# A fourth PSUM bank for the first experts' chunk, and squares of y that read SBUF

## The chip, the cores and the metric

One core of one Trainium2 chip. The metric is device time in microseconds (us) of one execution; the median of three runs of the kernel before is 762.8 us (761.18 to 762.97). Engines: PE is TensorE, DVE is VectorE, ACT is ScalarE, POOL is GpSimd, SP is SyncE, which issues nearly all DMAs.

## What is computed

```python
def reference(q, k, v, M_prev, z_prev, beta, w_in, w_out, domain_probs, w1, w2):
    # B, H, S, D = 2, 8, 576, 64
    attn = g * mem_out + (1 - g) * softmax(causal(q @ k.T / 8)) @ v     # g = sigmoid(beta)
    x = attn.transpose(0, 2, 1, 3).reshape(1152, 512)
    y = relu(x @ w_in) ** 2 @ w_out                                      # 512 -> 2048 -> 512
    p = domain_probs / domain_probs.sum(-1, keepdims=True)
    return sum(p[:, e:e+1] * (relu(y @ w1[e]) @ w2[e]) for e in range(4))  # 512 -> 1024 -> 512
```

## The kernel before, in words

The 1152 tokens are nine tiles of 128. The feed-forward layer in the middle (`ffn1`) takes them in three chunks: two tiles (c = 0), four tiles (c = 1), three tiles (c = 2). While chunk 0 runs, the attention of the other tiles is finished in between (`mix`), and so on; chunk 2 runs with the preparation of the experts. The values are kept as a high part and a low part (`xy[:, 0]`, `xy[:, 1]`), and products take three passes, high by high, high by low, low by high.

In `ffn1` the hidden units go in 16 blocks `f`: `up(f)` makes `hp` (12 matmuls, L89), ACT and DVE make the squared ReLU (L676, L677) and split it (L679, L680), `down(f)` adds to four PSUM accumulators `yacc` (L687). Behind the last block each accumulator is copied to `xy` by ACT (L693: the high part), subtracted by DVE (L694: the low part), and its squares are summed by ACT (L696, into `ysq`), from which a power-of-two scale for the experts is made later.

The experts are two chunks: c = 0 with tiles 0 to 3, c = 1 with tiles 4 to 8; each goes through 4 experts in 4 pairs of blocks, 16 pairs per chunk (`pairs`). A pair's first layer, `up2(i)`, is a seven-product (Strassen) form: for k = 0, 1, 4, 3, 5, 2, 6 in this order, `product(k)` makes six matmuls into one PSUM bank (L895), and ACT (L918, L924: k = 0 and 3) or DVE (L916, the other five) reads it. `hidden` then makes the ReLU's high part on ACT (L910) and its low part on DVE (L911). The second layer, `down2(i - 1)`, of the pair before is mixed in between: eight groups of three matmuls (L989) into the accumulators `o`. The order is two products, then a group of `down2`, a product, and so on. So each pair's first `down2` group needs the first `hidden` of the pair before, which comes from product 2, the last but one.

Which bank a product gets is set by `bank`: a counter goes up by one at each call, and its rest by three picks one of three PSUM tiles of one buffer each. A product can start when the product three calls before has been read. The two small sums `yt` and `wt` (L773) take a turn in the same rotation. The other five of the eight banks are `o0` to `o4`, in a pool `ps_o` that opens behind the first layer; the first expert chunk, of four tiles, uses `o0` to `o3`.

TensorE's instructions stand in the order in which the program writes them. Those of ACT, DVE, POOL and SP are put in order by a scheduler of the framework when the kernel is built, from its own estimates, so an edit can change their order far away from it. Each engine runs its instructions strictly in that order, and a wait blocks all behind it.

Of the kernel before, what the change touches and what calls it, by code (L numbers as in the profile page):

```python
# [10 lines left out]
F32 = mybir.dt.float32  # L11
# [5 lines left out]
AF = mybir.ActivationFunctionType  # L17
# [4 lines left out]
P = 128  # L22
B, H, S, D = 2, 8, 576, 64
DM = 512
NK = DM // P
# [27 lines left out]
def attention_then_experts(ctx, tc, qa, ka, va, qc, kc, vc, mz, beta, w1, probs, w2, out):  # L53
# [11 lines left out]
    nc = tc.nc  # L65
# [6 lines left out]
    ps_h = ctx.enter_context(tc.tile_pool(name="ps_h", bufs=1, space=PSUM))  # L72
# [5 lines left out]
    xy = xyp.tile([P, 2, NK, NTOK], F32R, name="xy")  # L78
# [41 lines left out]
    ysq = const.tile([P, 3, NK], F32, name="ysq")  # L120
# [3 lines left out]
    gp = kvs.enter_context(tc.tile_pool(name="gp", bufs=2))  # L124
# [516 lines left out]
    def ffn1(c, ps, gp, nh, cv=None):  # L641
        t0, t1 = CHUNKS[c]
        n, cs = (t1 - t0) * P, slice(t0 * P, t1 * P)
# [12 lines left out]
        def prep(f, half):  # L656
            if c == 0:
                while (f, half) not in made:
                    next(cv)
                raw = made.pop((f, half))  # L660
                next(cv, None)
            else:
                fetch(1)
                raw = raws.pop((f, half))
            w = wp.tile([P, 2, DM], F32R, tag=f"w{half}", name=f"w{half}")
            on_vector = ((f % 4 == 3, f % 4 == 3), (f < 3, f % 4 == 3), (False, f % 2))[c][half]
            split(w, raw, nc.vector if on_vector else nc.gpsimd)
            ws[f, half] = w
            fetch(2)
# [13 lines left out]
        def down(f):  # L683
            w, g = ws.pop((f, 1)), gs.pop(f)
            for d in range(NK):
                for i, (a, b) in enumerate(PASS):
                    nc.tensor.matmul(  # L687
                        yacc[d], lhsT=w[:, a, d * P:(d + 1) * P], rhs=g[:, b],
                        start=(f == 0 and i == 0 and d % per == 0),
                        stop=(f == n1 - 1 and i == 2 and d % per == per - 1),  # L690
                    )
                for k in range(d - per + 1, d + 1) if f == n1 - 1 and d % per == per - 1 else ():
                    nc.scalar.activation(out=xy[:, 0, k, cs], in_=yacc[k], func=AF.Copy)  # L693
                    nc.vector.tensor_sub(xy[:, 1, k, cs], yacc[k], xy[:, 0, k, cs].bitcast(F32))  # L694
                    junk = gp.tile([P, n], F32, tag="r", name="junk")
                    nc.scalar.activation(out=junk, in_=yacc[k], func=AF.Square, accum_out=ysq[:, c, k:k + 1])  # L696
                yield

        prep(0, 0)
# [2 lines left out]
        yacc = [banks[d // per][:, d % per, :] for d in range(NK)]  # L702
        for f in range(n1 + 2):
            if f + 1 < n1:
                prep(f + 1, 0)
            if 1 <= f <= n1:
                prep(f - 1, 1)
            if f < n1:
                yield from up(f)
            if f >= 2:  # L710
                yield from down(f - 2)

    with ExitStack() as ca:
        kva = ca.enter_context(tc.tile_pool(name="kva", bufs=1))
# [38 lines left out]
    ps_e = ctx.enter_context(tc.tile_pool(name="ps_e", bufs=1, space=PSUM))  # L753
    pairs = [(c, e, p) for c in range(2) for e in range(ne) for p in range(4)]
    width = [(t1 - t0) * P // 2 for t0, t1 in EXPERT_CHUNKS]
    xs, raws, wus, wds, gs = {}, {}, {}, {}, {}
    turn = [0]
# [3 lines left out]
    wsq = xp.tile([P, ne, 2, 4], F32, name="wsq", bufs=1)  # L761
    junk2 = xp.tile([P, 2 * DM], BF16, name="junk2", bufs=1)

    def bank(shape, name):
        turn[0] += 1
        pool, tag = ((ps_h, "h"), (ps_e, "b"), (ps_e, "d"))[turn[0] % 3]
        return pool.tile(shape, F32, tag=tag, name=name)

    def whole_sum(out, parts, acc):
# [74 lines left out]
    def fetch(i, half):  # L844
        if i < len(pairs):
            _, e, p = pairs[i]
            raw = raws[i, half] = xp.tile([P, 2 * DM], F32, tag=f"raw{half}", name=f"raw{half}", bufs=6 + half)
            nc.sync.dma_start(out=raw, in_=w2[e * 4 + p, half])
# [114 lines left out]
    ps_o = ctx.enter_context(tc.tile_pool(name="ps_o", bufs=1, space=PSUM))  # L963
# [45 lines left out]
                r += n  # L1009

    side = iter(())
    for i in range(len(pairs)):

        fetch(i + 6, 0)
        fetch(i + 6, 1)
        todo = iter([(j, half) for j in {0: (), 1: (4, 5), 2: (6, 7)}.get(i, (i + 5,)) for half in range(2)])
        if i:
            late = [down2(i - 1)] * (2 * (EXPERT_CHUNKS[pairs[i - 1][0]][1] - EXPERT_CHUNKS[pairs[i - 1][0]][0]))
            steps = spread([up2(i)] * 7, late, 0.25)
        else:  # L1020
            steps = []
        ahead = chain(prep_down(i), prep_up(i + 1))
        for n, g in enumerate(steps):
            next(g)
            next(ahead, None)
            if n in (5, 7, 9, 11):
                square(*next(todo, (len(pairs), 0)))
            if n == 10 and i == 1:
                y_power(1, bank([P, NK], "yt"))
                side = tokens(1, nc.vector)  # L1030
            if n == 14 and i < 4 * ne - 4 and i % 4 == 2:
                w_power(pairs[i + 2][1], bank([P, 8], "wt").rearrange("p (m n) -> p m n", m=2))
        if i >= 5 and steps:
            next(side, None)
        run(ahead)
# [61 lines left out]
```

## Time and profile before

| | |
|---|---|
| median of three runs | 762.8 us |
| the profiled execution | 762.13 us, its span from first to last instruction 760.1 us |
| PE busy | 706.0 us (93%) |
| DVE busy | 584.4 us (77%) |
| ACT busy | 448.6 us (59%) |
| POOL busy | 293.6 us (39%) |
| mean granted TensorE clock | 0.974 of full |

The span has these stretches: attention and first-layer chunk 0 to 152 us; chunk 1 with the last attention tiles to 301; chunk 2 with the experts' preparation to 389; experts' chunk 0 to 555; experts' chunk 1 to the end. Matmuls are pipelined, so PE's busy time is a union that covers overlaps; where PE was idle, the list of waits says what it waited for. The granted clock is 1.00 at 2.4 GHz and 0.50 at 1.2 GHz.

### The profile page before, as it was taken

To read this page: it belongs to the slowest core of one execution; us is meant where nothing else is said; L and a number is where in the kernel's file an instruction comes from. 1 tells how busy PE (TensorE), PEld (TensorE's weight loads), DVE (VectorE), ACT (ScalarE), POOL (GpSimd) and SP (SyncE) were. 2 spreads that over 40 slices of the span, in tenths; PEclk is the share of its full clock that TensorE was granted. 3 is DMA by queue.
4 is the path that set the end of the run, shared out by engine and by line. 5 is a ranking of instruction groups with operands and counts; after the bars stand their busy time and mean duration, and the time that the engine had idled before them with its cause. 6 is when DMAs were issued, how large, how long until landed. Compare 5 with 4: busy or idle time off the path is not lost.

```text
span 760.1 us, 12986 instructions
## 1 busy us (share of the span) xinstructions
PE 706.0 (93%) x4740; PEld 511.6 (67%) x4740; DVE 584.4 (77%) x1082; ACT 448.6 (59%) x878; POOL 293.6 (39%) x293
## 2 busy tenths in 40 slices
PE   6969999979999998989989898989999999999997
PEld 4758888867777886978866555656655555555553
DVE  4789998889989865566777679988777776776763
ACT  4679988785765545586766557645543534435341
POOL 1136645454533246744531324533333142332400
PEclk9979999999999999999989999999999999999999
DMA  9568776287885543685412322332333323100002
GB/s 241 172 231 281 245 249 231 91 272 215 178 209 125 114 111 91 209 289 167 139 57 66 101 88 87 104 108 92 124 121 113 92 75 111 56 1 1 1 1 69
DMA packets 65424, 101.28 MB, mean 133 GB/s; under 512 B 32656, under 2 KB 34704, under 8 KB 65360
## 3 DMA queue, kind: packets, MB, share of 16 engines
q1 hardware_dynamic: 65216, 100.45, 43.5%
q8 instruction: 37, 0.61, 0.3%
q14 instruction: 27, 0.22, 0.1%
q10 hardware_dynamic: 144, 0.00, 0.0%
HBM read 82.87 MB, written 10.75 MB: 123 GB/s over the span
## 4 chain that ended last, share of the span: by engine, by line
PE 55%; DVE 21%; ACT 9%; issue 7%; POOL 3%; DMA 3%; SPq 1%; DVEq 0%; POOLq 0%; ACTq 0%
PE o L989 18%; PE pe L895 16%; PE y L687 6%; PE hpb L89 3%; PE hpc L89 3%; DVE wu L859 2%; DVE bits L634 2%; PE pv L555 2%; DVE bits L631 2%; DVE a L172 2%; POOL w L83 1%; PE hpa L89 1%; PE sc L487 1%; PE sc L278 1%; DMA raw<-in_w 1%
## 5 line engine op out<-in xcount | busy, mean ns | idle before, releaser
L989 PE MATMUL o<-w,g 128*128 128x512 f16 x864 | 220.4, 383 | 6.2 <-ACT junk L696 2.2
L895 PE MATMUL pe<-xs,wu 128*128 128x256 f16 (+1 forms) x1344 | 200.6, 289 | 5.8 <-DVE h L916 5.7
L895 PEld LDWEIGHTS <-wu 128*128 128x128 f16 x1344 | 132.5, 99 | 76.6 <-issue 9.8
L989 PEld LDWEIGHTS <-g 128*128 128x128 f16 x864 | 84.8, 99 | 76.9 <-issue 4.3
L687 PE MATMUL y<-g,w 128*128 128x256 f32 (+2 forms) x576 | 124.1, 348 | 1.3 <-POOL w L83 0.7
L83 POOL TENSOR_TENSOR w<-wraw,w 128x512 fp32r<-128x512 f32 x49 | 72.2, 1475 | 107.2 <-ACT w L82 106.1
L910 ACT ACTIVATE g<-h 128x512 f16<-128x512 f32 (+1 forms) x64 | 43.4, 678 | 108.6 <-DVE h L916 108.4
L687 PEld LDWEIGHTS y<-g,w 128*128 128x128 f32 x576 | 93.8, 190 | 11.7 <-POOL w L83 0.9
L925 POOL TENSOR_TENSOR u<-u,p 128x256 f32<-128x256 f32 (+1 forms) x32 | 30.2, 944 | 126.2 <-ACT p L924 115.9
L862 POOL TENSOR_TENSOR ws<-raw 128x256 f32<-128x256 f32 x32 | 24.7, 772 | 117.5 <-issue 89.9
L911 DVE SCALAR_TENSOR_TENSOR g<-h,g 128x512 f16<-128x512 f32 (+1 forms) x64 | 50.5, 788 | 21.9 <-ACT g L910 21.7
L916 DVE SCALAR_TENSOR_TENSOR h<-pe,u 128x256 f32<-128x256 f32 (+1 forms) x96 | 43.1, 451 | 24.9 <-PE pe L895 17.9
L89 PE MATMUL hpb<-xy,w 128*128 128x512 f32 x192 | 53.9, 417 | 7.5 <-DVE r L677 5.8
L859 DVE SCALAR_TENSOR_TENSOR wu<-ws,wpow,wu 128x512 f16<-128x512 f32 x64 | 50.0, 819 | 3.6 <-ACT wu L870 3.6
L795 DVE SCALAR_TENSOR_TENSOR w<-raw,wpow,w 128x512 f16<-128x512 f32 x64 | 48.1, 754 | 0.7 <-ACT w L794 0.6
L89 PEld LDWEIGHTS hpb<-xy,w 128*128 128x128 f32 x192 | 36.5, 198 | 17.3 <-DVE r L677 8.3
L172 DVE CUSTOM_DVE_ANT_0 a<-sc,mask 128x384 f32<-128x384 f32 (+4 forms) x80 | 36.4, 476 | 13.4 <-PE sc L487 6.5
L89 PE MATMUL hpc<-xy,w 128*128 128x384 f32 x192 | 40.9, 361 | 6.1 <-POOL w L83 2.5
L82 ACT ACTIVATE w<-wraw 128x512 fp32r<-128x512 f32 x64 | 39.6, 624 | 11.0 <-PE y L687 8.8
L83 POOL TENSOR_TENSOR w<-bits,w 128x512 fp32r<-128x512 f32 x24 | 35.4, 1480 | 25.4 <-ACT w L82 25.4
L794 ACT ACTIVATE w<-raw,wpow 128x512 f16<-128x512 f32 x64 | 45.1, 709 | 0.1
L89 PE MATMUL hpa<-xy,w 128*128 128x256 f32 x192 | 35.7, 313 | 7.5 <-ACT mag L627 7.5
(160 smaller groups left out, 1268.6 us busy)
## 6 DMA issues: line engine op xcount, KB each, us to landing
raw<-in_w SPq DMA_DIRECT2D x64, 512.0 KB, 3.5
w<-in_w SPq DMA_DIRECT2D x32, 512.0 KB, 4.4
wraw<-w1s SPq DMA_DIRECT2D x64, 256.0 KB, 2.9
w1s<-bits SPq DMA_DIRECT2D x32, 256.0 KB, 2.4
kraw<-in_kc SPq DMA_DIRECT2D x8, 576.0 KB, 4.1
vraw<-in_vc SPq DMA_DIRECT2D x8, 320.0 KB, 3.4
qraw<-in_qc SPq DMA_DIRECT2D x4, 512.0 KB, 4.2
out<-acc SPq DMA_DIRECT2D x8, 256.0 KB, 2.1
```

The costliest lines, as they stand in the source:

```text
L83: eng.tensor_sub(w[:, 1], raw, w[:, 0].bitcast(F32))
L89: nc.tensor.matmul(acc, lhsT=w[:, a, kk * P:(kk + 1) * P], rhs=xy[:, b, kk, t0:t0 + n], start=(i == 0), stop=(i == 3 * NK - 1),)
L172: nc.vector.tensor_tensor_reduce(out=dst, in0=sc, in1=msk, op0=ALU.add, op1=ALU.max, scale=1.0, scalar=-3.0e38, accum_out=m)
L687: nc.tensor.matmul(yacc[d], lhsT=w[:, a, d * P:(d + 1) * P], rhs=g[:, b], start=(f == 0 and i == 0 and d % per == 0), stop=(f == n1 - 1 an ...
L794: nc.scalar.activation(out=w0, in_=x, func=AF.Copy, scale=s)
L795: nc.vector.scalar_tensor_tensor(out=w1, in0=x, scalar=s, in1=w0, op0=ALU.mult, op1=ALU.subtract)
L859: nc.vector.scalar_tensor_tensor(out=w[:, 1, ks], in0=x, scalar=s1, in1=w[:, 0, ks], op0=ALU.mult, op1=ALU.subtract)
L895: nc.tensor.matmul(acc, lhsT=w[:, wa, k, kk * P:kk * P + P], rhs=x[:, xb, kk], start=(m == 0), stop=(m == 5))
L910: nc.scalar.activation(out=g[:, 0], in_=hm, func=AF.Relu)
L911: nc.vector.scalar_tensor_tensor(out=g[:, 1], in0=hm, scalar=0.0, in1=g[:, 0], op0=ALU.max, op1=ALU.subtract)
L916: nc.vector.scalar_tensor_tensor(out=out, in0=acc, scalar=HID, in1=x, op0=ALU.mult, op1=ALU.add)
L989: nc.tensor.matmul(outs[t], lhsT=g[:, gb, r:r + P], rhs=w[:, wa], start=(p == 0 and m == 1 and k == 0), stop=(p == 3 and m == 0 and k == 2),)
```

## The change

The squares leave the loop over the accumulators and come behind it, as the last thing of the chunk; they read the high part of y in SBUF in place of the accumulator in PSUM. And the rotation gets a fourth tile, `o4` of `ps_o`, from the first pair of the expert loop until the second chunk begins.

```diff
                 for k in range(d - per + 1, d + 1) if f == n1 - 1 and d % per == per - 1 else ():
                     nc.scalar.activation(out=xy[:, 0, k, cs], in_=yacc[k], func=AF.Copy)
                     nc.vector.tensor_sub(xy[:, 1, k, cs], yacc[k], xy[:, 0, k, cs].bitcast(F32))
-                    junk = gp.tile([P, n], F32, tag="r", name="junk")
-                    nc.scalar.activation(out=junk, in_=yacc[k], func=AF.Square, accum_out=ysq[:, c, k:k + 1])
                 yield
...
             if f >= 2:
                 yield from down(f - 2)
+        for k in range(NK):
+            junk = gp.tile([P, n], F32, tag="r", name="junk")
+            y = xy[:, 0, k, cs].bitcast(F32)
+            nc.scalar.activation(out=junk, in_=y, func=AF.Square, accum_out=ysq[:, c, k:k + 1])
...
+    spots = [(ps_h, "h"), (ps_e, "b"), (ps_e, "d")]
+
     def bank(shape, name):
         turn[0] += 1
-        pool, tag = ((ps_h, "h"), (ps_e, "b"), (ps_e, "d"))[turn[0] % 3]
+        pool, tag = spots[turn[0] % len(spots)]
         return pool.tile(shape, F32, tag=tag, name=name)
...
     side = iter(())
+
+    spots.append((ps_o, "o4"))
     for i in range(len(pairs)):
+        if pairs[i][0] and len(spots) > 3:
+            spots.pop()
```

TensorE's order is the same in both kernels. The scheduler's order changes on the other engines; in the changed kernel the squares are line 713, and lines behind it have other numbers (L910 is L914, L911 is L915, L918 is L922, L864 is L868).

On ACT, at the end of first-layer chunk 1 (y_1997 to y_2000 are the four accumulators, tp a transposed tile of attention whose copy L199 the next chunk's first product reads; L82 copies a weight):

```order
 L693 ACTIVATE xy<-y_1997 128x512
+L713 ACTIVATE junk,ysq<-xy 128x512
 L693 ACTIVATE xy<-y_1998 128x512
 L693 ACTIVATE xy<-y_1999 128x512
-L696 ACTIVATE junk,ysq<-y_1997 128x512
-L696 ACTIVATE junk,ysq<-y_1998 128x512
-L696 ACTIVATE junk,ysq<-y_1999 128x512
 L199 ACTIVATE xy<-tp 128x4x128
 L693 ACTIVATE xy<-y_2000 128x512
+L713 ACTIVATE junk,ysq<-xy 128x512 x3
 L82 ACTIVATE w_3780<-wraw 128x512
-L696 ACTIVATE junk,ysq<-y_2000 128x512
```

Three squares stood ahead of the copy of tp; one stands there now, between the first two accumulators, and three stand behind the last accumulator's copy, ahead of the weight.

On ACT, at the end of first-layer chunk 2 and the start of the experts, the kernel before (y_3706 to y_3709 are the accumulators, g the first pair's hidden parts, p of pe a product's copy, wu weights):

```order
L693 ACTIVATE xy<-y_3706 128x384
L696 ACTIVATE junk,ysq<-y_3706 128x384
L910 ACTIVATE g_4506<-h_4428 128x512
L693 ACTIVATE xy<-y_3707 128x384
L910 ACTIVATE g_4524<-h_4427 128x512
L693 ACTIVATE xy<-y_3708 128x384
L693 ACTIVATE xy<-y_3709 128x384
L696 ACTIVATE junk,ysq<-y_3707 128x384
L918 ACTIVATE p_4582<-pe 128x256
L864 ACTIVATE wu<-raw_3874,wpow 128x768
L696 ACTIVATE junk,ysq<-y_3708 128x384
L696 ACTIVATE junk,ysq<-y_3709 128x384
```

and the changed kernel in the same place:

```order
L693 ACTIVATE xy<-y_3706 128x384
L713 ACTIVATE junk,ysq<-xy 128x384
L693 ACTIVATE xy<-y_3707 128x384
L914 ACTIVATE g_4504<-h_4428 128x512
L713 ACTIVATE junk,ysq<-xy 128x384
L693 ACTIVATE xy<-y_3708 128x384
L693 ACTIVATE xy<-y_3709 128x384
L914 ACTIVATE g_4520<-h_4427 128x512
L713 ACTIVATE junk,ysq<-xy 128x384 x2
L922 ACTIVATE p_4582<-pe 128x256
L868 ACTIVATE wu<-raw_3874,wpow 128x768
```

The last reading of an accumulator on ACT was a square behind a product's copy and a weight's; it is now the copy of y_3709, and the last two squares stand ahead of the product's copy.

On DVE, early in first-layer chunk 1 (L677 reads hpb and makes the squared ReLU, L166 and L167 belong to the attention's phi, L447 to its keys kst, L466 to its values vct):

```order
 L680 TENSOR_TENSOR g<-r,g 128x512
+L677 SCALAR_TENSOR_TENSOR r<-hpb,r 128x512
 L166 TENSOR_SCALAR phi<-phi 128x1024
-L677 SCALAR_TENSOR_TENSOR r<-hpb,r 128x512
 L167 SCALAR_TENSOR_TENSOR qraw<-qraw,phi 128x1024
-L466 SCALAR_TENSOR_TENSOR vct<-vraw,vs,vct 128x640
-L680 TENSOR_TENSOR g<-r,g 128x512
-L466 SCALAR_TENSOR_TENSOR vct<-vraw,vs,vct 128x640
-L447 TENSOR_TENSOR kst<-kraw,kst 64x576
+L680 TENSOR_TENSOR g<-r,g 128x512
+L466 SCALAR_TENSOR_TENSOR vct<-vraw,vs,vct 128x640 x2
 L677 SCALAR_TENSOR_TENSOR r<-hpb,r 128x512
```

One L677 moves ahead of L166, and the next L677 ahead of a subtraction for the keys. Some 20 rows further on both orders run alike again.

## Rows read from the trace of the kernel before

**Rows 1.** PE's list of waits: waiter, releaser, us in total, times, longest.
```profile
PE pe L895 <- DVE h L916: 5.7, 7, 1.6
...
PE o L989 <- DVE g L911: 2.1, 5, 0.9
...
PE hpb L89 <- ACT junk L696: 1.4, 1, 1.4
```

**Rows 2.** Windows: length, busy PE PEld DVE ACT POOL, granted clock, DMA share, GB/s.
```profile
450.00:490.00 40.00, 37.26 (x238) 23.80 (x237) 39.85 (x73) 27.29 (x45) 16.38 (x17) 0.96 0.31 97
510.00:750.00 240.00, 240.00 (x1458) 142.44 (x1457) 175.34 (x293) 105.45 (x162) 72.29 (x97) 1.00 0.20 66
```

**Rows 3.** The same view, of stretches right behind single waits of PE.
```profile
392.20:395.60 3.40, 3.40 (x13) 1.62 (x12) 2.62 (x7) 0.31 (x1) 0.75 (x2) 0.51 0.52 160
303.50:306.90 3.40, 3.40 (x12) 3.40 (x11) 0.81 (x2) 0.69 (x2) 0.00 (x0) 0.50 0.46 136
504.90:508.30 3.40, 3.09 (x12) 1.72 (x12) 3.33 (x14) 1.51 (x3) 0.00 (x0) 0.50 0.02 5
436.40:439.80 3.40, 3.40 (x22) 2.13 (x23) 3.40 (x7) 3.19 (x7) 0.00 (x0) 1.00 0.00 0
```

**Rows 4.** Timeline, chunk 1 begins: start, length, instruction, idle before and its releaser.
```profile
164.15 1.04 ACT L164 ACTIVATE phi<-qraw 128x1024 f32<-128x1024 f32 x1
165.10 0.58 ACT L676 ACTIVATE r<-hpb 128x512 f32<-128x512 f32 x1
166.15 0.69 DVE L166 TENSOR_SCALAR phi<-phi 128x1024 f32<-128x1024 f32 x1
167.49 4.35 PE L89 MATMUL hpb<-xy,w 128*128 128x512 f32 x12 [2.71 <-DVE r L677]
...
174.73 1.72 DVE L447 TENSOR_TENSOR kst<-kraw,kst 64x576 fp32r<-64x576 f32 x1
177.22 1.65 PE L89 MATMUL hpb<-xy,w 128*128 128x512 f32 x3 [1.57 <-DVE r L677]
```

**Rows 5.** Timeline where chunk 1 ends and chunk 2 begins.
```profile
300.07 0.59 ACT L696 ACTIVATE junk<-y 128x512 f32<-128x512 f32 x1
301.78 0.61 ACT L199 ACTIVATE xy<-tp 128x512 fp32r<-128x512 f32 x1
302.45 0.44 PE L89 MATMUL hpc<-xy,w 128*128 128x384 f32 x1 [1.77 <-ACT xy L199]
```

**Rows 6.** Timeline where chunk 2 ends and the experts begin.
```profile
389.02 1.01 DVE L694 TENSOR_TENSOR xy<-y,xy 128x384 fp32r<-128x384 f32 x2
390.86 0.53 ACT L696 ACTIVATE junk<-y 128x384 f32<-128x384 f32 x1
391.53 0.81 PE L989 MATMUL o<-w,g 128*128 128x512 f16 x3 [2.23 <-ACT junk L696]
```

**Rows 7.** Timeline between the tenth and the eleventh expert pair of chunk 0.
```profile
503.03 0.41 DVE L916 SCALAR_TENSOR_TENSOR h<-pe,u 128x256 f32<-128x256 f32 x1
503.49 0.81 PE L895 MATMUL pe<-xs,wu 128*128 128x256 f16 x6 [1.23 <-DVE h L916]
504.13 0.69 DVE L911 SCALAR_TENSOR_TENSOR g<-h,g 128x512 f16<-128x512 f32 x1 [0.70 <-ACT g L910]
505.21 1.44 PE L895 MATMUL pe<-xs,wu 128*128 128x256 f16 x6 [0.91 <-DVE h L916]
506.45 1.48 PE L989 MATMUL o<-w,g 128*128 128x512 f16 x3
```

**Rows 8.** Timeline between the fourth and the fifth pair of chunk 0.
```profile
434.98 0.82 PE L895 MATMUL pe<-xs,wu 128*128 128x256 f16 x6 [0.83 <-DVE h L916]
...
436.37 0.60 PE L989 MATMUL o<-w,g 128*128 128x512 f16 x2 [0.34 <-DVE g L911]
```

**Rows 9.** Timeline where the experts' chunk 1 begins.
```profile
554.85 0.42 DVE L916 SCALAR_TENSOR_TENSOR h<-pe,u 128x256 f32<-128x256 f32 x1
554.87 1.79 PE L895 MATMUL pe<-xs,wu 128*128 128x320 f16 x12
```

## The prediction, made before the changed kernel ran

> **What bounds the kernel now.** I read PE's list of waits first, since PE is busy 93% of the span. These of its entries touch the change: 5.7 us in which a product waits for a bank that DVE has not read [rows 1]; 1.4 and 2.23 us in which PE waits for a square (L696) to let go of an accumulator's bank [rows 1, 6]; 1.77 us for the copy of tp, which stands behind squares on ACT [rows 5]; and 2.1 us in which a `down2` group waits for DVE's hidden part [rows 1]. Next the windows: from 510 to 750 us PE is busy 240 of 240 us at full clock [rows 2], so whatever PE gains ahead of 510 arrives at the end undiminished. From 450 to 490 DVE is busy 39.85 of 40 us [rows 2]: there DVE is the bound, not PE, and a bank for PE buys nothing as long as DVE's queue is full. The third view is the clock: right behind the waits of 2.23, 1.77 and 1.23 + 0.91 us stand 3.4 us at 0.50 to 0.51 of full clock; behind the waits that end at 434.98 and 436.37, of 0.83 us for a bank and 0.34 us for `g`, it stayed at 1.00 [rows 3, 5 to 8]. A stretch of 3.4 us at half clock does 1.7 us less work: that is the price of one.
>
> **The change, part by part.**
>
> *Squares, end of chunk 0.* PE waits 1.4 us for a square [rows 1]; the accumulators' last readers are now copies and subtractions that no square precedes by more than one, so this wait should go. It does not arrive in full, since PE then waits for DVE twice: 2.71 and 1.57 us [rows 4]. What counts is when L677 runs. On ACT its input L676 (165.10) stood behind L164 (164.15, 1.04 us) and now stands ahead of it; on DVE L677 takes the place of L166, which began at 166.15. So PE resumes about 0.6 us earlier than 167.49 (L166's issue-to-issue time). The next L677 loses L447 (1.72 us) ahead of it and gets L166 (0.6 us) in its stead: 0.6 + 1.72 - 0.6 = 1.7 us earlier, and as PE itself comes 0.6 earlier, its wait of 1.57 us shrinks to about 0.5. **Gain 1.7 us**; below, 0.6 if L447's place is taken by another late input; above, 3.4 if the half clock behind the second wait goes too. L447 itself comes later; the scores that need those keys belong to the next group of heads and have the whole of this group's work to cover it. Without that cover each would cost its 1.72 us.
>
> *Squares, end of chunk 1.* L199 ran at 301.78, behind three squares from 300.07 on: 0.57 us each [rows 5]. Two of them go behind it. The third stays ahead, now between the first two copies, and I count it in full. Gain 1.71 - 0.57 = 1.14, at most 1.7; I take **1.2 us**. PE's wait falls from 1.77 to about 0.6 us and the half clock at 303.5 [rows 3] should go: **1.7 us** more. The cost: three squares (1.7 us) now stand ahead of a weight copy L82 in chunk 2. That weight is for a `down` two blocks of `up` later (a block's 12 matmuls, 512 columns wide, took 4.35 us [rows 4]), so it is hidden; if not, 1.7 us.
>
> *Squares, end of chunk 2.* PE's first `down2` waits for the last square, at 390.86; `ps_o` reuses the accumulators' banks. Now the last reader is DVE's last subtraction, and the pair of these ended at 389.02 + 1.01 = 390.03 [rows 6]. So PE starts 391.53 - 390.03 = **1.5 us** earlier (at most 2.2, the whole wait), with a wait of about 0.7 us left, and the half clock at 392.2 [rows 3] goes: **1.7 us**. The two squares in front of the first product's copy delay it by about 1.1 us; the product's bank is not needed for four more products, so this is hidden.
>
> *The price of a square.* It reads SBUF in place of PSUM. The trace has 0.59 us for 512 columns from PSUM [rows 5] and 1.04 us for 1024 from SBUF [rows 4], so an estimate for 512 from SBUF lies between 0.52 (half) and 0.6; I take no difference. Twelve squares at 0.05 us either way are 0.6 us on an engine that is not the bound.
> The Trainium skill (Perfetto Trace Analysis, "Optimizing Scalar/DVE Operations") speaks against this part: it gives ScalarE about 93 ns of access overhead on SBUF against 51 on PSUM. By it the twelve would cost an estimated 0.5 us more of ACT time; the rows show no such excess, and the sum would be the same by either, as the squares now stand behind what PE waits for.
>
> *The fourth bank.* A product can start when the one four calls before has been read. Of the 5.7 us, the waits ahead of 500 us give nothing: those from 450 on lie where DVE is full [rows 2], and the one at 434.98 is followed by a `down2` group that waits for a hidden part all the same [rows 8]. What counts is the last one, since PE never waits after it. At 503 PE's two products waited 1.23 and 0.91 us, and the `down2` group began at 506.45 [rows 7]. With four banks the first runs before 503, the second at 503.45, when L916 (503.03 + 0.41) has read its bank; then the group waits for L911, which ends at 504.82. So it starts 506.45 - 504.82 = **1.6 us** earlier, with two idle pieces of about 0.9 and 0.5 us in place of 1.23 and 0.91. These are nearer to 0.83 and 0.34 [rows 8] than to the ones that halved the clock, so I take the half clock at 504.9 as gone: **1.7 us**. Bounds: nothing, if DVE's queue is as late as PE is early, to 5.0, if the half clock that rows 1's longest wait (1.6 us) left at 460 comes back to PE too.
>
> *Back to three banks.* Up to then the counter has been called 16 x 7 times for products, once for `yt` and three times for `wt`: 116. Call 117 takes tile 0 of three; call 116, just ahead of it, took tile 0 of four. So the first product of chunk 1 waits for the last read of chunk 0, right before it: L916 there runs from 554.85 to 555.27, PE began at 554.87 [rows 9]: **0.4 us lost**, up to 1.0.
>
> *Sum.* 1.7 + 1.2 + 1.7 + 1.5 + 1.7 + 1.6 + 1.7 - 0.4 = 10.7 us. It is made against the profiled execution, 762.13 us (span 760.1 and 2.0 around it), so 751.4; that execution was 0.7 us below the median of 762.8, so the median is forecast at **752.1 us**.
>
> **Rivals.** A measurement of this kernel tells about 0.3% from no change, 2.3 us.
>
> *The clock does not come back.* The half clock may hang on more than the waits that I shorten: what is left (0.6, 0.7, 0.9 + 0.5 us) may be enough, or another place halves it instead. Then the three 1.7 go and 10.7 - 5.1 = 5.6 us are left: 757.2 us. For it: 2.14 us in two pieces with work between were enough at 503. Against it: 0.83 and 0.34 were not.
> The Trainium skill (TensorE: Matmul & The Clock Gate, "HAM oscillation — how this bites in real kernels") names only idle gaps longer than any of these as what halves the clock; by it the halves here are not the waits' doing and would stay, which is this rival's 757.2. The trace disagrees: all three stand right behind a wait.
>
> *The bank only moves the wait.* DVE is full from 450 on; PE, early by what it gained before, then waits longer for `g`, and the clock halves behind that wait. Then 1.6 + 1.7 go and one more half clock comes, 1.7: 10.7 - 5.0 = 5.7, or 757.1 us.
>
> *More.* The half clock behind the second wait of chunk 1 goes (1.7) and the bound of 5.0 for the bank holds (1.7 more): 748.7 us.
>
> *Nothing arrives.* A stage between 390 and 450 follows its own chain (weights, their DMAs, the ReLU behind a square of a weight that waits for its DMA) and takes up what chunks 0 to 2 gained, so that only the bank's 3.3 less 0.4 is left of it, and half of that: within 0.3%, 761.4.
>
> *Slower.* The scheduler put keys and values of the attention later in chunk 1. If the scores wait for L447 in each of the three later groups of heads, with 1.72 us and a half clock of 1.7 each, that is 10.3 us and the forecast is gone; from four such waits, 13.7 us, the kernel is 3.0 us slower, 765.8. Against it: both orders run alike again some 20 rows on.
>
> **How the numbers follow.** Forecast 0.48, the clock 0.17, the bank 0.13, more 0.10, nothing 0.07, slower 0.05. The first four are all faster: 0.88; same 0.07; slower 0.05. The forecast's own range, from its bounds, is 749 to 755. The range of 747 to 759.5 takes in "more" and both rivals at 757 with 2 us for the uncertain terms of chunk 1, and leaves out the last two.
>
> **What would show it.** PE's list of waits without L696 or its successor; L199's wait near 0.6 us; the wait ahead of the first `down2` near 0.7; clock 1.00 behind each of these; `pe` waiting for DVE less than 2 us in all, `o` for `g` more than before; a wait of about 0.4 us at the first product of the experts' second chunk. Wrong would make it: a half clock where I took it away, new waits in chunk 1 on kst or vct, or DVE idle between 450 and 500.

## The result, and the profile after

The changed kernel took 753.18 us (median of 4 runs, 751.68 to 754.7), beside 761.99 us for the kernel before (median of 4); the ratio is 0.9893 with a 95% interval from 0.9858 to 0.9929, 8.1 us less. The forecast was 752.1 us, "faster" with a chance of 0.88. Time and sign came out. The runs below show that one of the two causes in the forecast's sum did not deliver: the squares brought all of it, the fourth bank nothing that can be measured.

The first view is PE's list of waits, of the changed kernel (waiter, releaser, us in total, times, longest).

```profile
PE o L993 <- DVE g L915: 5.3, 9, 1.3
...
PE hpb L89 <- DVE r L677: 4.8, 2, 3.6
PE pe L899 <- DVE h L920: 3.0, 5, 1.3
...
PE o L993 <- ACT g L914: 2.4, 4, 1.0
...
PE hpc L89 <- ACT xy L199: 0.3, 1, 0.3
```

No square is a releaser any more, and the wait for the copy of tp fell from 1.77 us [rows 5] to 0.3. The products' wait for a bank fell from 5.7 us to 3.0, of which 1.3 is a single wait at 382.16, ahead of the first `down2` group; behind that group it is 1.7. But the wait of the `down2` groups for DVE's half of `g` rose from 2.1 [rows 1] to 5.3 us. What was taken from one line of the list stands in another.

The second view is PE's timeline at the places of [rows 4 to 7] and [rows 9] (start, length, instruction, idle before it and what ended that).

```profile
166.25 4.59 PE L89 MATMUL hpb<-xy,w 128*128 128x512 f32 x12 [3.65 <-DVE r L677]
...
174.56 0.96 PE L89 MATMUL hpb<-xy,w 128*128 128x512 f32 x3
...
302.35 0.44 PE L89 MATMUL hpc<-xy,w 128*128 128x384 f32 x1 [0.27 <-ACT xy L199]
303.30 1.49 PE L89 MATMUL hpc<-xy,w 128*128 128x384 f32 x7 [0.51 <-DVE xy L200]
...
382.16 0.82 PE L899 MATMUL pe<-xs,wu 128*128 128x256 f16 x6 [1.29 <-DVE h L920]
...
387.79 0.81 PE L993 MATMUL o<-w,g 128*128 128x512 f16 x3
...
496.71 0.82 PE L899 MATMUL pe<-xs,wu 128*128 128x256 f16 x6 [0.81 <-DVE h L920]
...
498.10 0.61 PE L993 MATMUL o<-w,g 128*128 128x512 f16 x2 [0.34 <-DVE g L915]
...
546.27 0.98 PE L899 MATMUL pe<-xs,wu 128*128 128x320 f16 x6 [0.29 <-DVE h L920]
```

At the start of chunk 1 two waits for a square and L677 became one of 3.65 us, and the second wait for L677 (1.57 us, [rows 4]) is gone. The first `down2` group starts at 387.79 instead of 391.53 [rows 6] with no wait to speak of. Of the pair of bank waits at 503 [rows 7] one is left, 0.81 us, followed by one of 0.34 us for `g`.

The third view is that of windows (length, busy PE, PEld, DVE, ACT, POOL, granted clock, DMA share, GB/s).

```profile
292.90:299.70 6.80, 6.80 (x37) 5.51 (x36) 0.69 (x1) 1.71 (x4) 3.50 (x3) 0.51 0.05 20
...
387.70:391.20 3.50, 3.46 (x23) 2.15 (x22) 2.95 (x6) 2.97 (x7) 0.00 (x0) 1.00 0.04 5
450.00:490.00 40.00, 35.50 (x234) 22.43 (x234) 39.72 (x71) 29.17 (x48) 19.50 (x19) 1.00 0.29 93
...
510.00:740.00 230.00, 229.70 (x1387) 135.37 (x1386) 169.46 (x283) 100.89 (x155) 69.77 (x92) 1.00 0.20 65
```

The half clocks at 303.5, 392.2 and 504.9 [rows 3] are gone and the experts' first chunk runs at full clock throughout. But there is a half clock that was not there before: 6.8 us from 292.9 on, behind waits of 0.95 and 0.54 us that both kernels have.

For all that follows, one table. It gives the time between PE groups that every kernel has, in us, each the difference of two start times in that kernel's own trace (`hpb` and `hpc` are `hp` of chunks 1 and 2): from the first `hpb` to the last, to the first `hpc`, to the last `hpc`, to the first `o`, to the first product of the experts' second chunk. "Half" is the time at a granted clock of 0.50 from the first `hpb` to that product. Where PE is busy all the time, 3.4 us of it do 1.7 us less work; how much of that arrives at the end differs from place to place, as the table shows.

| kernel | chunk 1 | its end | chunk 2 | its end | experts' chunk 0 | half |
|---|---|---|---|---|---|---|
| before | 133.2 | 17.3 | 70.5 | 18.6 | 163.3 | 27.3 |
| changed | 132.1 | 18.7 | 69.0 | 16.4 | 158.5 | 17.1 |
| changed, again (5) | 131.1 | 18.7 | 68.9 | 16.4 | 158.9 | 20.5 |
| bank only (1) | 133.9 | 17.3 | 69.6 | 18.6 | 160.2 | 20.5 |
| squares only (2) | 131.6 | 18.8 | 68.9 | 16.4 | 159.0 | 17.1 |
| squares late, PSUM (3) | 132.6 | 15.6 | 70.5 | 18.6 | 163.0 | 20.5 |
| squares in loop, SBUF (4) | 131.4 | 18.0 | 70.7 | 16.4 | 159.4 | 20.5 |
| u4 on DVE, four banks (6) | 131.3 | 18.8 | 69.2 | 16.4 | 155.1 | 20.5 |
| u4 on DVE, three banks (7) | 131.2 | 18.8 | 68.9 | 16.4 | 154.9 | 20.5 |
| tokens on POOL (8) | 131.2 | 18.8 | 69.7 | 16.4 | 164.0 | 27.3 |
| u4, tokens on POOL (9) | 131.1 | 18.8 | 69.1 | 16.4 | 160.5 | 27.3 |
| zeros at 287 (10) | 132.1 | 15.9 | 68.5 | 16.8 | 155.2 | 3.4 |
| zeros at 162 (11) | 139.0 | 15.2 | 68.5 | 16.8 | 155.1 | 10.2 |
| zeros at 287 and 197 (12) | 131.3 | 15.9 | 68.2 | 16.8 | 155.0 | 10.2 |

Where the first `hpb` itself stands (149.2 to 151.9 us) differs by up to 2.7 us between executions; nothing of the change lies ahead of it.

Two things in the table bear on all that follows. First, a half clock of 3.4 us near 375 (378.6 before, also in runs 1, 3 to 9 and 12) costs nothing: chunk 2's end takes 16.4 us in the changed kernel's two traces, with it in the second and without it in the first, which waits 1.29 us for a bank there instead (382.16 above). Second, run 10 has 17.1 us less of half clock than run 7, at 1.7 us for each 3.4 a gain of 8.5, and its five stretches are 1.7 us shorter in sum: the end of chunk 1 gained 2.9, the others lost 1.2 in sum.

### The profile page after: what moved, and what is told of

Read it like the earlier page. It is cut to its first block, busy times and chain, and to the rows that moved or that the text cites. A ratio compares the mean times of both kernels' runs of the same rounds, so it can differ in the third digit from the quotient of the medians.

```text
span 751.7 us, 12979 instructions
## 1 busy us (share of the span) xinstructions
PE 701.8 (93%) x4740; PEld 509.7 (68%) x4740; DVE 584.9 (78%) x1082; ACT 448.0 (60%) x878; POOL 298.1 (40%) x293
## 4 chain that ended last, share of the span: by engine, by line
PE 51%; DVE 22%; ACT 9%; issue 8%; DMA 6%; POOL 3%; SPq 1%; DVEq 0%; ACTq 0%; POOLq 0%
PE o L993 17%; PE pe L899 15%; PE y L687 6%; PE hpb L89 3%; DMA raw<-in_w 3%; PE pv L555 2%; DVE bits L634 2%; DVE wu L863 2%; DVE bits L631 2%; DVE w L799 2%; PE hpa L89 1%; DVE g L915 1%; DVE a L172 1%; PE sc L278 1%; DMA qa<-in_qa 1%
## 5 line engine op out<-in xcount | busy, mean ns | idle before, releaser
L899 PE MATMUL pe<-xs,wu 128*128 128x256 f16 (+1 forms) x1344 | 196.8, 286 | 3.0 <-DVE h L920 3.0
L687 PE MATMUL y<-g,w 128*128 128x256 f32 (+2 forms) x576 | 127.7, 356 | 1.3 <-POOL w L83 0.7
L914 ACT ACTIVATE g<-h 128x512 f16<-128x512 f32 (+1 forms) x64 | 43.4, 678 | 108.0 <-DVE h L920 107.8
L687 PEld LDWEIGHTS y<-g,w 128*128 128x128 f32 x576 | 96.5, 194 | 12.2 <-POOL w L83 0.9
L929 POOL TENSOR_TENSOR u<-u,p 128x256 f32<-128x256 f32 (+1 forms) x32 | 32.8, 1026 | 134.0 <-ACT p L928 120.1
L915 DVE SCALAR_TENSOR_TENSOR g<-h,g 128x512 f16<-128x512 f32 (+1 forms) x64 | 50.8, 793 | 21.6 <-ACT g L914 21.4
L82 ACT ACTIVATE w<-wraw 128x512 fp32r<-128x512 f32 x64 | 39.5, 622 | 11.2 <-PE y L687 8.6
L795 ACT ACTIVATE junk<-raw 128x1024 bf16<-128x1024 f32 x32 | 33.5, 1048 | 16.4 <-DMA raw<-in_w 16.2
L89 PE MATMUL hpc<-xy,w 128*128 128x384 f32 x192 | 38.5, 345 | 4.8 <-POOL w L83 2.5
```

Source lines behind the costliest of these rows:

```text
L89: nc.tensor.matmul(acc, lhsT=w[:, a, kk * P:(kk + 1) * P], rhs=xy[:, b, kk, t0:t0 + n], start=(i == 0), stop=(i == 3 * NK - 1),)
L687: nc.tensor.matmul(yacc[d], lhsT=w[:, a, d * P:(d + 1) * P], rhs=g[:, b], start=(f == 0 and i == 0 and d % per == 0), stop=(f == n1 - 1 an ...
L899: nc.tensor.matmul(acc, lhsT=w[:, wa, k, kk * P:kk * P + P], rhs=x[:, xb, kk], start=(m == 0), stop=(m == 5))
L914: nc.scalar.activation(out=g[:, 0], in_=hm, func=AF.Relu)
L915: nc.vector.scalar_tensor_tensor(out=g[:, 1], in0=hm, scalar=0.0, in1=g[:, 0], op0=ALU.max, op1=ALU.subtract)
```

## The experiments

**1 to 4: the two parts apart, and the two sides of the squares' part.** Run 1 is the kernel before with the change to `spots` alone; run 2 the change without this line:

```diff
-    spots.append((ps_o, "o4"))
```

Run 3 moves the squares behind the loop, but they go on reading PSUM; run 4 lets them read SBUF where they stood. Both have three banks.

```diff
# run 3, behind the loop
+            nc.scalar.activation(out=junk, in_=yacc[k], func=AF.Square, accum_out=ysq[:, c, k:k + 1])
# run 4, in the loop
-                    nc.scalar.activation(out=junk, in_=yacc[k], func=AF.Square, accum_out=ysq[:, c, k:k + 1])
+                    nc.scalar.activation(out=junk, in_=xy[:, 0, k, cs].bitcast(F32), func=AF.Square, accum_out=ysq[:, c, k:k + 1])
```

Run 1: 

> Only the fourth bank; the squares stay as in the kernel before. The forecast's terms: 1.6 + 1.7 - 0.4 = 2.9 us faster than before (ratio 0.996), with the waits up to the first down2 group of the experts unchanged and only the half clock near 505 us gone. What the trace after suggests (8.4 us in all, of which 3.7 had arrived at the first down2 group): 4.7 us faster (0.994), with the half clocks near 460 and 505 both gone. If the bank only moves the wait from the bank to g: within 0.5 us of before. If the gain of the bank needs the squares' gain ahead of it: under 2 us.

Run 2: 

> Only the squares; three banks throughout. The forecast's terms: 1.7 + 1.2 + 1.7 + 1.5 + 1.7 = 7.8 us faster (ratio 0.990), the end of the first layer 7.8 us earlier. What the trace after suggests: the first down2 group comes 3.7 us earlier, and that arrives undiminished at the end (0.995), half clocks near 460 and 505 as before. If what PE gains ahead of 390 us is taken up by waits for banks in the experts' first chunk: under 2 us.

Run 3: 

> The squares stand behind the copies of all blocks but still read the accumulators in PSUM; three banks. If the gain comes from the place of the squares on ACT alone: the same as the squares of the change, within 1 us. If it comes from the banks that they let go of: PE still waits for squares at the end of chunk 0 (1.4 us or more) and ahead of the first down2 group (2.2 us or more, half clock behind it), and only the copy of tp at 302 us comes earlier; the gain is then that of chunk 1 alone, at most 1.2 + 1.7 = 2.9 us, and nothing if the waits at the two other ends grow with the four squares now at the end of the row.

Run 4: 

> The squares read SBUF but stand where they stood in the code, behind the copy of each block; three banks. The scheduler then puts two squares more ahead of the copy of tp at the end of chunk 1 than in the change and, at the end of chunk 0 and 2, one at most at another place. If the banks that are let go of are what counts: the same as the squares of the change, less what the copy of tp loses: two squares of 0.57 us, wait near 1.4 us, and a half clock of 1.7 us behind it if the length of the wait decides (2.8 us less gain in all). If the place counts at all three ends: no gain over before.

Measured beside 761.79 us for before: bank only 760.53 us (ratio 0.998 [0.996, 1.0]); squares only 751.62 us (0.9878 [0.9851, 0.9905]); squares late from PSUM 756.85 us (0.9936 [0.9912, 0.996]); squares in the loop from SBUF 752.92 us (0.9893 [0.9863, 0.9923]).

The squares alone give all that the change gives. What the bank does is seen in PE's waits of run 1, and beside it of run 2:

```profile
PE o L991 <- DVE g L913: 5.2, 9, 1.3
...
PE o L991 <- ACT g L912: 2.4, 4, 1.0
...
PE pe L897 <- DVE h L918: 1.8, 4, 0.8
```

```profile
PE pe L899 <- DVE h L920: 6.8, 7, 1.6
...
PE o L993 <- DVE g L915: 2.2, 5, 0.9
...
PE o L993 <- ACT g L914: 1.1, 2, 0.7
```

Run 2's 6.8 us, too, have a wait of 1.3 ahead of the first `down2` group. Counted from behind that group's start to the second chunk, the waits for a bank and for `g` add up to 8.8 us with three banks (5.5 + 2.2 + 1.1) and to 9.4 and 9.7 in the two traces of the changed kernel, with four; without the squares' change to 9.7 before and 9.4 in run 1. So the bank moves the wait to `g` one for one. In the table, the experts' chunk 0 takes 159.0 us in run 2 and 158.5 and 158.9 in the changed kernel. Run 1's 160.2 against 163.3 is no clean comparison: the one trace of the kernel before has three half clocks there, run 1's has one.

The half clocks of the kernel before at 460 and 505 are not bound to three banks either. Four kernels have the bank waits of 0.7 + 1.6 and of 1.2 + 0.9 us that stand there (before and runs 2 to 4). Near the first pair of waits the clock halved in two of them (before and run 2), behind the second in two (before and run 3).

Runs 3 and 4 tell the two sides of the squares' part apart, and each counts at a place of its own. The source weighs more: reading SBUF in the old place (run 4) gave 8.2 us of the 9.3, the new place with PSUM (run 3) 4.9. At the end of chunk 2 the source decides: in run 3 PE still waits there, as before [rows 6].

```profile
387.26 0.81 PE L992 MATMUL o<-w,g 128*128 128x512 f16 x3 [2.23 <-ACT junk L712]
```

At the end of chunk 1 the place decides. In run 3 the copy of tp has no square ahead of it and the first `hpc` waits for nothing; in run 4, with two more squares ahead of that copy than in the change, it waits 1.59 us:

```profile
298.13 0.44 PE L89 MATMUL hpc<-xy,w 128*128 128x384 f32 x1
```

```profile
299.06 0.44 PE L89 MATMUL hpc<-xy,w 128*128 128x384 f32 x1 [1.59 <-ACT xy L199]
```

At the end of chunk 0 PE waited for no square in run 3 either, against the expectation. Run 3's 4.9 us (by its interval 3.0 to 6.7) lie between the two theories. Its five stretches are 2.6 us shorter than before, 1.7 of it at the end of chunk 1, within the 2.9 that the second allowed; another 2.0 of its trace lie ahead of the first `hpb`, where executions differ.

Run 1 shows something of the clock besides. It has the same wait of 1.77 us as before [rows 5], and behind it the clock stayed at 1.00:

```profile
302.72 0.44 PE L89 MATMUL hpc<-xy,w 128*128 128x384 f32 x1 [1.77 <-ACT xy L199]
```

```profile
303.60:307.00 3.40, 3.40 (x21) 3.40 (x22) 1.70 (x4) 2.10 (x6) 0.21 (x1) 1.00 0.37 135
```

**5 to 8: why the bank buys nothing.** Waits for `g` in its place say that the chain from a product to `g` is late. One part of that chain is `u4`, a sum that goes into both hidden halves. In the changed kernel's trace, all engines, around one of the longest of them:

```profile
424.89 0.36 ACT L928 ACTIVATE p<-pe 128x256 f32<-128x256 f32 x1
...
426.33 0.72 POOL L929 TENSOR_TENSOR u<-u,p 128x256 f32<-128x256 f32 x1
...
427.08 0.42 DVE L920 SCALAR_TENSOR_TENSOR h<-pe,u 128x256 f32<-128x256 f32 x1 [2.61 <-POOL u L929]
...
428.74 0.41 DVE L920 SCALAR_TENSOR_TENSOR h<-pe,u 128x256 f32<-128x256 f32 x1
...
429.19 0.63 ACT L914 ACTIVATE g<-h 128x512 f16<-128x512 f32 x1 [1.61 <-DVE h L920]
...
429.87 0.39 PE L993 MATMUL o<-w,g 128*128 128x512 f16 x1 [1.02 <-ACT g L914]
```

u4 goes from PSUM over ACT and then stands on POOL behind three adds for weights; DVE idles 2.61 us for it. So at 425 us DVE is not the bound; whether it is from 450 to 490, where the forecast read its busy share [rows 2], is a question of its own. Runs 6 and 7 (four and three banks) make u4 on DVE from the bank itself; run 8 takes work off DVE instead; run 5 is the change once more.

```diff
-        nc.scalar.activation(out=p5, in_=product(3), func=AF.Copy, scale=HID)
-        nc.gpsimd.tensor_add(u4, u2, p5)
+        add(u4, product(3), u2)
# run 8 (without the above)
-                side = tokens(1, nc.vector)
+                side = tokens(1, nc.gpsimd)
```

Run 5: 

> The changed kernel once more, timed beside the next three. If the bank adds 2.9 us to the squares, as forecast, the ratio to before is 0.003 to 0.004 below that of the squares alone (0.9878). If it only moves PE's waits from the bank to g: the same as the squares alone within 1 us, waits for a bank near 3 us and for g near 7.7 us in the experts' first chunk, against 6.8 and 3.3 there. Where the half clocks stand should be the same as in the first trace if the waits ahead of them set it; if the same waits are followed by it in one execution and not in another, a single trace can't price them.

Run 6: 

> The change, and u4 made on DVE straight from the product's bank (0.42 us a pair) in place of a copy on ACT and an add on POOL. If g is late because u4 goes over ACT and POOL (1.8 us from the product's end to u4 at 425 us, where DVE stood idle for 2.61 us): PE's waits for g fall from 7.7 us to under 3, the stage from the first down2 group to the experts' second chunk from 158.5 to 155 us or less, and the kernel is 3 to 5 us faster than the change (ratio to before 0.983 to 0.985). If DVE is the bound there (39.85 of 40 us from 450 to 490): 16 more operations of 0.42 us on it in that chunk, the waits stay, and it is 0 to 4 us slower than the change.

Run 7: 

> As the last, with three banks. If the fourth bank was worth nothing only because g was late: here PE still waits for the bank (5 us or more), and this is 2 to 3 us slower than the same with four banks. If the bank is worth nothing in either case: the two agree within 1 us.

Run 8: 

> The change, with the four sums of the second chunk's tokens (0.90 us each, 128x640) on POOL in place of DVE. If DVE, full from 450 to 510 us, sets the waits there: 3.5 us less for it, 1 to 3 us faster than the change. If g is late by u4's way over POOL: no change within 1 us, or slower, since u4 then stands behind these sums on POOL.

Measured beside 760.86 us: the change again 751.79 us (0.9887 [0.9847, 0.9927]), level with the squares alone, with 1.7 us of waits for a bank and 8.0 for `g` in the experts' first chunk; u4 on DVE 749.13 us with four banks (0.9851 [0.9816, 0.9886]) and 748.45 us with three (0.9847 [0.981, 0.9884]); tokens on POOL 757.67 us (0.9964 [0.9937, 0.9991]).

Run 7's chain, at the same place of the program, has no POOL in it, and the second of the two `h` above (428.74 there) starts at 424.22. `g` starts at 424.77, 4.4 us ahead of the 429.19 above, of which 1.6 us are the lead that it already had at the first `o`.

```profile
424.22 0.42 DVE L920 SCALAR_TENSOR_TENSOR h<-pe,u 128x256 f32<-128x256 f32 x1
...
424.77 0.61 ACT L914 ACTIVATE g<-h 128x512 f16<-128x512 f32 x1
```

The experts' chunk 0 falls to 155 us in all runs with this edit that leave the tokens on DVE (6, 7 and 10 to 12 in the table), though DVE carries 16 operations more there. Where it is won, and where a bank's lead is lost, shows in the starts of single `down2` stages: the first matmul into `o` of a pair, in us behind the first of all.

| kernel | 4th stage | 7th | 9th | 11th | second chunk |
|---|---|---|---|---|---|
| squares only, three banks (2) | 30.3 | 67.0 | 87.4 | 111.5 | 159.0 |
| changed, again, four banks (5) | 30.5 | 64.4 | 87.4 | 110.0 | 158.9 |
| u4 on DVE, four banks (6) | 30.6 | 61.2 | 84.2 | 106.8 | 155.1 |
| u4 on DVE, three banks (7) | 30.1 | 62.9 | 84.0 | 107.3 | 154.9 |

The windows of run 5, and then of run 6, that belong to the 4th to 7th stage and to what follows:

```profile
416.00:450.00 34.00, 30.52 (x200) 19.42 (x200) 27.05 (x46) 20.68 (x37) 11.24 (x14) 1.00 0.28 93
450.00:490.00 40.00, 35.83 (x235) 22.49 (x233) 39.72 (x72) 29.02 (x49) 18.80 (x18) 1.00 0.29 98
```

```profile
416.00:450.00 34.00, 32.04 (x214) 20.53 (x213) 29.11 (x54) 22.31 (x39) 9.38 (x12) 1.00 0.27 93
450.00:490.00 40.00, 35.44 (x232) 22.26 (x231) 39.87 (x74) 25.92 (x41) 12.02 (x15) 1.00 0.30 103
```

The u4 edit wins its 3.2 us between the 4th and the 7th stage, where DVE is busy 27.05 of 34 us and had waited for u4; from there to the 11th both kernels take 45.6 us, with DVE at 99% from 450 to 490 in either. So the way over ACT and POOL was the bound ahead of 450 us. Whether its length counts or the load that it put on ACT and POOL is not told apart.

The bank gives PE a lead of 2.6 us by the 7th stage (1.7 with u4 on DVE). By the 9th it is gone in both pairs of kernels: from the 7th to the 9th stage four banks take 23.0 us, three 20.4 and 21.0, with DVE at 99 to 100% in all four. With four banks PE is idle for 2.8 us there, nearly all of it for DVE's half of `g`. That DVE's full queue takes the lead back is read from these traces; the runs that were to relieve DVE (8 and 9) did not. Behind the 11th, a second lead of 1.5 us goes the same way to 0.1. So the bank is worth nothing even with u4 on DVE, 749.13 us with it and 748.45 without: waits for a bank fall from 2.5 us to 0.6, those for `g` rise from 3.9 to 6.0. Run 6's expectation of less than 3 us of them, and run 7's of 5 us or more for a bank, were misses.

Run 8 took the sums off DVE and yet lost 5.9 us against run 5. One sum took 1.53 to 1.98 us on POOL, where one takes 0.90 on DVE, and DVE, which works in order, waits for it with the experts' work behind:

```profile
482.35 1.98 POOL L815 TENSOR_TENSOR tt<-xy 128x640 f32<-128x640 f32 x1
```

```profile
DVE tt L833 <- POOL tt L815: 2.8, 1, 2.8
...
DVE xs L799 <- ACT xs L798: 2.4, 3, 1.6
```

```profile
440.10 0.39 PE L993 MATMUL o<-w,g 128*128 128x512 f16 x1 [2.59 <-ACT g L914]
...
489.08 0.39 PE L993 MATMUL o<-w,g 128*128 128x512 f16 x1 [2.43 <-ACT g L914]
```

**9: the same relief with u4 off POOL** (both edits above, three banks). 

> Squares, three banks, u4 on DVE, and the four sums of the second chunk's tokens on POOL, where u4 no longer stands. If DVE is the bound of the experts' first chunk once u4 is off POOL: 2 to 4 us faster than the same with these sums on DVE (748.45 us). If these sums' own way over POOL, which takes longer for one, makes the second chunk's tokens or POOL's adds for the weights late: no change or slower.

Measured beside 762.22 us, as runs 10 and 11: 754.11 us (0.9894 [0.9865, 0.9922]), by the ratios 0.0047 or 3.6 us more than run 7. PE's wait for ACT's half of `g` was 5.7 us, of which 2.3 once, and DVE waited 3.0 us once for a sum on POOL. That sum is late with or without u4 beside it. What a true relief of DVE would give stays open.

**10 to 12: the half clocks.** If PE's idle time is what halves the clock, work without effect in it should keep it up. `idle` adds products with a tile of zeros (made once, at the start, on ACT) to an accumulator; in run 10 six, ahead of the pv group (attention times values) with the waits of 0.95 and 0.54 us; in run 11 fourteen, ahead of the hpb group with the wait of 3.67 us; in run 12 the six and eight more ahead of a pm group at 197. All have three banks and u4 on DVE, so run 7 is what they compare with.

```diff
+        def idle(acc, times):
+            for _ in range(times):
+                nc.tensor.matmul(acc, lhsT=zero, rhs=xy[:, 0, 0, cs], start=False, stop=False)
...
# runs 10 and 12, in down
+                if c == 1 and f == n1 - 2 and d == 1:
+                    idle(yacc[d], 6)
# run 11, in up
+            if c == 1 and f == 3:
+                idle(yacc[3], 14)
# run 12, in down
+                if c == 1 and f == 4 and d == 1:
+                    idle(yacc[d], 8)
```

Run 10: 

> Squares, three banks, u4 on DVE, and six matmuls of zeros (128x512, about 0.23 us each) added to an accumulator ahead of the pv group at 287 us, in which PE waits 0.95 + 0.54 us and behind which the clock stood at 0.50 for 6.8 us in most of the traces with the squares from SBUF. If PE's idle time there is what halves the clock: the half clock near 290 is gone, the first product of chunk 2 comes 3.4 us earlier, and the kernel is 3 us faster than without (748.45 us). If something else halves it (the short matmuls behind the wait, the load of the whole chip): it stays, and the kernel is the same within 1 us. The values are unchanged, as zeros are added.

Run 11: 

> The same with fourteen matmuls of zeros ahead of the hpb group at 165.6 us, where PE waits 3.67 us and the clock then stood at 0.50 for 6.8 us, in place of those at 287. Their 3.3 us lie in the wait. The scheduler takes them for a delay and puts some operations of ACT and DVE between 170 and 220 us in another order. If PE's idle time halves the clock: the half clock near 164 is gone and the kernel is 2 to 3.4 us faster than without (748.45 us). If not: it stays, and the same within 1 us.

Run 12: 

> As the kernel with six matmuls of zeros at 287 us (744.95 us), and eight more (128x512, about 1.9 us) ahead of the pm group at 196 us, in which PE waits 2.11 us for a copy of ACT and behind which the clock stood at 0.50 for 3.4 us in four of the traces. If PE's idle time halves the clock: no half clock between 195 and 210, and up to 1.7 us faster than without these eight, less in the median as not every execution has this half clock. If PE's group was not held by that copy alone, or the two rows of ACT that change places there make the next softmax late: no change, or up to 2 us slower.

Measured: run 10 744.95 us (0.9791 [0.9758, 0.9823]), by the ratios 0.0056 or 4.3 us less than run 7, which was timed in another session; run 11 752.54 us (0.9883 [0.9853, 0.9914]), 2.7 us more than run 7; run 12 745.33 us beside 762.34 (0.9799 [0.9775, 0.9823]). First run 7's windows, then run 10's timeline and windows:

```profile
164.40:171.20 6.80, 5.61 (x13) 4.46 (x14) 6.76 (x7) 2.94 (x5) 4.32 (x3) 0.51 0.82 290
290.70:297.50 6.80, 6.80 (x48) 5.62 (x47) 0.03 (x1) 1.51 (x3) 2.99 (x3) 0.51 0.09 33
```

```profile
164.30 3.02 PE L89 MATMUL hpb<-xy,w 128*128 128x512 f32 x12 [3.62 <-DVE r L683]
...
287.22 1.53 PE L675 MATMUL y<-xy,zero 128*128 128x512 f32 x6
288.68 0.25 PE L557 MATMUL pv<-vct,aht 128*64 128x64 f16 x2
```

```profile
164.30:171.10 6.80, 6.80 (x30) 5.32 (x30) 6.77 (x5) 5.08 (x7) 5.48 (x3) 1.00 0.69 245
289.00:295.80 6.80, 6.72 (x77) 5.69 (x78) 1.21 (x3) 2.48 (x5) 4.60 (x4) 1.00 0.17 41
```

With the zeros in place of the idle time, the half clock near 290 is gone, here and in run 12, and the end of chunk 1 takes 15.9 us instead of 18.8. The short matmuls behind it run at full clock now, so they are not what halved it; the idle time has a part in it. But in the same trace a wait of 3.62 us at 164.30, not filled, has no half clock behind it, where run 7's has 6.8 us. An idle piece is needed, but does not settle it.

Run 11 fills that wait, and the group behind it runs at full clock; but the scheduler, which takes the zeros for a delay, puts other work of ACT and DVE first, and the next hpb group waits 4.57 us:

```profile
162.40 3.37 PE L675 MATMUL y<-xy,zero 128*128 128x512 f32 x14
166.24 3.01 PE L89 MATMUL hpb<-xy,w 128*128 128x512 f32 x12 [0.47 <-DVE r L685]
...
177.62 1.65 PE L89 MATMUL hpb<-xy,w 128*128 128x512 f32 x3 [4.57 <-DVE r L685]
```

Run 12 has no half clock near 200 in its trace, as run 7 without zeros has none, but one of 6.8 us at 164, where run 10 had none; its time is that of run 10, and its chunk 1 takes no longer (131.3 us against 132.1). Run 10 stays the fastest version found: the squares of the change, three banks, u4 on DVE and six matmuls of zeros.

## Why the prediction was right, and where its sum was not

*Squares, end of chunk 0* (1.7 us, bounds 0.6 to 3.4). Right: L677 runs ahead of L166 and of L447, PE's second wait of 1.57 us is gone altogether. Chunk 1 took 1.1 us less in the first trace and 2.1 in the second; the half clock behind the first wait stayed.

*Squares, end of chunk 1* (1.2 us and a half clock of 1.7). The wait came out as said, 0.27 and then 0.51 us for 1.77. In the traces this end takes 1.4 us longer all the same, since 6.8 us of half clock stand in it now. Without them run 10 took 15.9 us, against 17.3 before: the wait was worth about 1.4 us. The half clock at 303.5 falls into chunk 2, which takes 70.5 us before and 69.6 in run 1, with the same wait and without the half clock: it was worth about 0.9. That it is sure to stand behind that wait was wrong.

*Squares, end of chunk 2* (1.5 us, at most 2.2, and 1.7). The whole 2.2 us: 16.4 instead of 18.6 in each of the runs whose squares read SBUF and that have no zeros. The half clock behind that wait stood in all three traces that have the wait (before, runs 1 and 3) and in none without, and was worth 1.7: the first pair of the experts takes 11.8 us with it and 10.1 without.

*The price of a square* (no difference). Too low, by little. For 512 columns of ACT's list, before and after (busy us, mean ns):

```profile
L696 ACT ACTIVATE junk<-y 128x512 f32<-128x512 f32 x4 | 2.3, 598 | 0.3 <-DVE xy L694 0.3
```

```profile
L713 ACT ACTIVATE junk<-xy 128x512 f32<-128x512 f32 x4 | 2.5, 642 | 0.0
```

With 512 to 524 ns for 384 columns and 382 to 412 for 256 that is 4 x (44 + 12 + 30) ns = 0.34 us for all twelve. The Trainium skill (Perfetto Trace Analysis, "Optimizing Scalar/DVE Operations") had the sign right; by its figures the estimate was 0.5.

*The fourth bank* (1.6 us and 1.7, less 0.4). **This is the step that failed**: "What counts is the last one, since PE never waits after it." The forecast rightly gave nothing for the waits from 450 on, where DVE is full. The lead at the last wait was sized well too: 1.5 us at the 11th stage for the 1.6 of the sum. But that PE never waits behind it is read from a trace with three banks, where PE comes late. With four it waits 0.34 and 0.24 us for `g` and 0.29 for the first product of the second chunk, and from the 11th stage on it takes 48.9 us instead of 47.5: 0.1 of the 1.5 is left. The half clock at 504.9 is gone with four banks, but it is missing in two of the four kernels with three as well (runs 2 and 4), so it is not shown to be the bank's. By itself the bank measured 1.3 us (760.53 beside 761.79; the interval goes from 0 to 3.0), on top of the squares nothing (0.9893 and 0.9887 beside 0.9878), with u4 on DVE nothing (749.13 and 748.45). The rival "the bank only moves the wait", at 0.13, had this mechanism and its reason, DVE's full queue; only its half clock behind the longer wait did not come.

*Back to three banks* (0.4 lost). Measured 0.29 us.

*The three half clocks* (5.1 us). All three are gone in both traces. They were worth about 0.9 us (303.5), 1.7 (392.2) and 1.7 (504.9: from the 11th stage to the second chunk run 3, with that half clock, takes 49.2 us, run 4, without it, 47.5). The new one at 290 took 2.9 of that back (18.8 us in run 7, 15.9 in run 10). The rival "the clock does not come back" (0.17) was half true: another place halved it.

So the squares were sized at 7.8 us and gave 9.3 (0.0122 of 762), the bank at 2.9 and gave nothing beside them. In run 2's trace the stretches up to the first `o` give 3.9 us and the experts' chunk 0 another 4.3, where the forecast had only the 1.7 of the half clock at 392 for the squares; of the 2.6 more, 1.7 are the half clock at 505, which the sum had put down to the bank. The errors are of opposite sign, and the sum of 10.7 stood against 8 to 9: that the time came so near is in part luck.

Nothing spoke for the rival "slower": no wait for kst or vct is new in PE's list. L447 now runs at 174.92, in 0.76 us.

## What to carry to other kernels

One more bank lets PE run ahead only as long as the engine that reads the banks and makes PE's next operand has room to follow. Before counting the gain of a wait that goes, look at the next operand that PE needs and at the engine that makes it: where DVE was 99% busy, PE's lead of 2.6 us was gone within two pairs. "PE never waits behind this" is true of the trace that it is read from, not of a kernel in which PE comes earlier.

A busy share says where to look, stretch by stretch. Ahead of 450 us DVE was 80% busy with idle pieces of up to 2.61 us in front of what mattered, and a detour's end made the kernel 3 us faster though DVE got 16 operations more; from 450 to 490 the same edit won nothing. Price a half clock by the time between two points of the program, in several executions: some here cost 1.7 us, some nothing, as PE would have waited anyway.

## What the runs showed of the hardware

The half clock does not follow from the length of the wait ahead of it. Waits of 3.6 to 3.7 us near 164 were followed by 6.8 us of it in runs 4 to 9 and 12, by 3.4 in the change's first trace and run 2, by none in run 10. The wait of 1.77 us at 302 was followed by it before and not in run 1. The waits of about 0.95 and 0.5 us at 290 were followed by it in all eight traces with the squares from SBUF that have both waits and no zeros (the change twice, runs 2, 4 and 6 to 9), and in none of those with the squares from PSUM (before, runs 1 and 3), though waits and matmuls are the same; run 11, where only the 0.95 us is left of the two, has none. Why is open.

With matmuls of zeros in the idle time no half clock followed at any place where that was tried: at 290 the clock was 1.00 in runs 10 and 12, against 0.51 in run 7. At 166 (run 11) and 197 (run 12) this shows less, since run 10 has none at 164 and run 7 none near 200 without zeros there. The Trainium skill (TensorE: Matmul & The Clock Gate, "HAM oscillation — how this bites in real kernels") names idle gaps longer than these as what halves the clock; the traces disagree, with 6.8 us at 0.51 behind 0.95 and 0.54 us of idle.

One 128x640 sum took 1.53 to 1.98 us on POOL and 0.90 on DVE; a 128x256 add on POOL took 0.72 us, and 1.30 in other places of the same trace.
